# Second FFN of a fused attention and two-FFN kernel: how its w_out part is interleaved, which engine takes the low parts, and where the last y tiles and late weight parts lie

## The chip, the core and the metric

One Trainium2 chip, one core. The time of a run is the device time of the whole program in microseconds (us); lower is better. Engines are named as in the profile: PE (TensorE matmul), PEld (its weight load), DVE (VectorE), ACT (ScalarE), POOL (GpSimd), SP (SyncE, which issues nearly all DMAs here).

## What is computed

```python
# attention on keys and values averaged over 8 rows, then:
def _moe_ref(x, w_in, w_out):                       # 4608 tokens, 512 -> 2048 -> 512
    h = x @ w_in
    g = np.maximum(0.01 * h, h)
    return (g @ w_out).astype(np.float32)

def _moe2_ref(x, w_gate, w_val, w_out, rms_g):      # 4608 tokens, 512 -> 1536 -> 512
    rms = np.sqrt(np.mean(x * x, axis=-1, keepdims=True) + 1e-06)
    xn = x / rms * rms_g
    g = xn @ w_gate
    silu = g * (1.0 / (1.0 + np.exp(-g)))
    val = xn @ w_val
    return (silu * val @ w_out).astype(np.float32)
```

The weights arrive as 64-bit numbers and are turned into 32-bit ones in the kernel.

## The kernel before, in words

**Precision.** Every fp32 operand is kept as two fp32r parts: `split` (L95, L98) lets ACT copy the high part and lets DVE or POOL subtract it from the source for the low part. A product is three matmuls: high by high, high by low, low by high (`TERMS`).

**Stages.** Attention and the first FFN run together for five blocks of 512 tokens. The other four blocks go through the first FFN as two pairs, and all tokens go through the second FFN as five pairs of 2x512 or 2x384 tokens (512, 384, 512, 384, 512). Pairs use a scheme of seven products instead of eight (`Quad`, `Second`): the tokens' sums are built by `token_steps` (sums and parts `T`, `xa`, `xb`), the weights' sums beforehand by `unit` and `late_unit`, which make parts, store them in DRAM (`op_g`, `op_v`, `op_o`) and load them again when used.

**A second-FFN pair** (`second_ffn`). Its first half is 6 x 14 steps of `Quad` (gate and value products); a step is six matmuls and one `spot()`, and `at_spot` hangs other work on numbered spots. `a = 14 * NPAIR` = 84 is the first spot of the second half, the **w_out part**: 42 steps `k`, seven products (A11, S2, S1, S3, A12, S4, A22) of six steps each. A step is 12 matmuls of 128x256 for a 512 pair and 9 for a 384 pair. Step `k` runs `product(k)`, `pump()` (weight loads), `combine(k + 4)` (DVE sums for S3 and A22, L1405 and L1408), `prepare(k + 3)` (ACT high part, then the low part on DVE for even k and on POOL for odd k; tiles `b`), and `spot()`. The `b` tiles have four buffers, so ACT can write the high part of k + 3 once product k - 1 is done. The last step of a product also calls `finish`: the sums of its two PSUM banks (`v` after S2, `z` with two sums a bank after S3, `v` after S4, `u` after A22, copies on ACT after A11 and A12) and the stores of the output. DVE, ACT and POOL each work strictly in program order.

In the same part the next pair's `token_steps` hang on spots a+6, a+9, ... a+33: two `first`, then `sums`, `second`, `second_more` for each of two chunks, then two `third`. Their x tiles were normalised by `norm_steps` in the first half (squares, `mean`, `root` with a matmul `ms` at L1040, reciprocals, scaling).

**Where the two FFNs meet.** The last w_out pieces of the first FFN (`y_part`, L1366 on PE, evacuated to `oe` tiles at L1373 and L1375) run between the first steps of the first second-FFN pair, and so do the last two `late_unit`s (tiles `parts_o`). Both take tiles of the pool tag `e` (nine buffers), which also holds the `e1`, `e6`, `e7` and `e2` tiles of `Quad`. The slots `"o"` (four) hold the first FFN's w_out blocks until their last use.

Of the kernel before, what the change touches and what calls it, by code (L numbers as in the profile page):

```python
# [9 lines left out]
F32 = mybir.dt.float32  # L10
# [7 lines left out]
HI, LO = 0, 1  # L18
# [5 lines left out]
def pooled_attention_then_two_ffns(  # L24
# [685 lines left out]
    ready = set()  # L710

    def side_steps():
# [123 lines left out]
        freed = []  # L836

        def late_unit(begin, n, name, out, src, srcs_of, zs):
# [12 lines left out]
            def high(i):  # L851
                held[i] = []
                for o, (x, dst) in enumerate(srcs_of(held["raw"])[i]):
                    a, b = x.shape[1:]
                    halves = [(x, dst)]
                    if b == 512:
                        halves = [
                            (x[:, :, c:c + 2 * P], dst.rearrange("p a (h n) -> p a h n", h=2)[:, :, :, c:c + 2 * P])
                            for c in (0, 2 * P)
                        ]  # L860
                    for k, (x, dst) in enumerate(halves):
                        t = p2.tile([P, 512], F32R, tag="e", bufs=9, name=f"parts_{name}_{i}_{o}_{k}")
                        d = t[:, :2 * a * x.shape[2]].rearrange("p (a h n) -> p a h n", a=a, h=2)
                        held[i].append((x, d, dst))
                        nc.scalar.activation(out=d[:, :, HI, :], in_=x, func=AF.Copy)
# [131 lines left out]
    def norm_steps(q):  # L997
# [8 lines left out]
        for z in range(2):  # L1006
# [51 lines left out]
            steps += [lambda c=c, f=square: f(c) for c in range(KC)] + [wait, mean, wait, wait, root, wait]  # L1058
# [300 lines left out]
    def y_part(q, z, f, ms):  # L1359
# [3 lines left out]
        for m in ms:  # L1363
# [6 lines left out]
            if f == blocks(q, z)[-1]:  # L1370
                t = e_tile(N, f"oe{q}_{z}_{m}")
                if m % 2:
                    nc.scalar.copy(out=t, in_=pt)  # L1373
                else:
                    nc.vector.tensor_copy(out=t, in_=pt)  # L1375
                nc.sync.dma_start(out=y_dram[j][:, m, :], in_=t)

    class Second:


        def __init__(self, q):
# [6 lines left out]
            self.e = {}  # L1388

# [20 lines left out]
        def prepare(self, k):  # L1410
# [12 lines left out]
            split(nc.scalar, t[:, HI, :], nc.gpsimd if k % 2 else nc.vector, t[:, LO, :], src)  # L1423

        def product(self, k):
            w, x, f = self.steps[k]
            to = {"A11": "x", "A12": "x", "S1": "w", "S4": "w"}.get(w, "y")
# [16 lines left out]
            if f == HF - 1:  # L1444
                for i in range(2):
                    self.finish(w, i, self.banks[to][i][:, :2 * P * min(2, nm - 2 * i)])
# [6 lines left out]
        def finish(self, w, i, pt):  # L1453
            n = pt.shape[1]
            e = self.e
            if w == "A11":
                nc.scalar.copy(out=self.tile("u", i, n), in_=pt)
            elif w == "S2":
                add(self.tile("v", i, n), pt, e["u", i])
            elif w == "S3":  # L1460
                add(self.tile("z", i, n), pt, e["u", i])
                add(e["z", i], self.banks["w"][i][:, :n], e["z", i])
                self.store(1, 1, i, e["z", i])
            elif w == "A12":
                nc.scalar.copy(out=self.tile("c", i, n), in_=pt)
                self.store(0, 0, i, e["c", i])
            elif w == "S4":
                add(e["v", i], pt, e["v", i])
                self.store(0, 1, i, e["v", i])
            elif w == "A22":  # L1470
                add(e["u", i], pt, e["u", i])
                self.store(1, 0, i, e["u", i])
# [246 lines left out]
    def second_ffn(q):  # L1719
# [16 lines left out]

        n = 0
# [19 lines left out]
        early, late = token_steps(q + 1, xs, True) if more else ([], [])  # L1757
        for k, f in enumerate(early + late):
            put(a + 6 + 3 * k, f)
        for k in range(len(second.steps)):  # L1760
# [4 lines left out]
            spot()  # L1765
        assert not at_spot

    for q, kind in enumerate(kinds):
# [3 lines left out]
        else:  # L1772
            second_ffn(q)
# [41 lines left out]
```

## Time and profile before

| | |
|---|---|
| median of 3 runs | 1819.7 us (1812.56 to 1821.94) |
| the profiled execution's own time | 1818.55 us |
| its span, first to last instruction | 1816.8 us |
| PE busy | 1738.1 us, 96% of the span |
| DVE, ACT, POOL busy | 62%, 43%, 40% |
| mean granted TensorE clock | 0.987 of full speed |

Busy time counts an instruction from its start to its end, also while it stands still for something inside it, so a busy engine need not be a working one. Matmul ends are modelled; their starts are better for measuring distances. In waits, `PE yo <- DVE b` means that PE sat idle until DVE had written `b`.

### The profile page before, as it was taken

What the parts mean: (1) busy time and instruction counts of PE and PEld (TensorE: products, weight loads), DVE (VectorE), ACT (ScalarE), POOL (GpSimd) and SP (SyncE); (2) the same over time, 40 slices, a digit from 0 to 9 for tenths busy, and PEclk for the clock granted to TensorE, in tenths of its full rate; (3) what the DMA queues carried; (4) which work ended last, traced back from release to release, by engine and by line L of the source; (5) the groups of instructions that cost most, each with busy time, mean ns of one, the idle gap of its engine ahead of it and who ended that gap; (6) DMA issues with size and microseconds to landing.
All of it is one profiled execution on the core that took longest, in us unless ns stands there. A gap on an engine that the chain in (4) does not pass through costs nothing.

```text
span 1816.8 us, 26931 instructions
## 1 busy us (share of the span) xinstructions
PE 1738.1 (96%) x9412; PEld 1518.6 (84%) x9412; DVE 1132.5 (62%) x1901; ACT 775.3 (43%) x1646; POOL 724.9 (40%) x842
## 2 busy tenths in 40 slices
PE   6899999999999999999999998999899989989999
PEld 5799888888888888777787888999788989978889
DVE  7984555655557444475675657577755765693455
ACT  5664444454454444444453324334332434341133
POOL 5632334555432133443463334334432533351144
PEclk9899999999999999999999999999999999999999
DMA  7543655556676599979896565768565657765563
GB/s 246 198 142 111 229 194 176 176 156 215 207 224 199 172 330 321 355 246 352 289 315 223 189 225 177 241 234 280 181 227 193 213 181 267 271 211 187 177 234 114
DMA packets 227446, 403.39 MB, mean 222 GB/s; under 512 B 59120, under 2 KB 137456, under 8 KB 226800
## 3 DMA queue, kind: packets, MB, share of 16 engines
q1 hardware_dynamic: 227312, 401.67, 66.2%
q8 instruction: 75, 1.23, 0.3%
q14 instruction: 59, 0.48, 0.1%
HBM read 320.34 MB, written 81.26 MB: 221 GB/s over the span
## 4 chain that ended last, share of the span: by engine, by line
PE 72%; DVE 14%; DMA 5%; ACT 3%; issue 2%; POOL 2%; SPq 1%; ACTq 0%; DVEq 0%; POOLq 0%
PE y L642 11%; PE h L597 10%; PE o L1366 7%; PE yv L1260 5%; PE yg L1260 5%; PE wv L1260 4%; PE xo L1436 4%; PE wg L1260 4%; PE yo L1436 4%; PE xg L1260 4%; PE xv L1260 3%; PE yh L1260 3%; PE wh L1260 2%; DVE b L98 2%; PE sc L322 2%
## 5 line engine op out<-in xcount | busy, mean ns | idle before, releaser
L597 PE MATMUL h<-xhl,w_i 128*128 128x512 f32 (+1 forms) x996 | 252.8, 396 | 4.7 <-DVE ghl L620 4.7
L597 PEld LDWEIGHTS h<-xhl,w_i 128*128 128x128 f32 x996 | 178.3, 192 | 35.3 <-DVE ghl L620 5.2
L98 POOL TENSOR_TENSOR b<-u,b 128x512 fp32r<-128x512 f32 (+1 forms) x90 | 125.4, 1398 | 97.9 <-ACT b L95 97.9
L95 ACT ACTIVATE b<-u 128x512 fp32r<-128x512 f32 (+1 forms) x180 | 102.6, 585 | 125.2 <-DVE u L1405 32.8
L642 PE MATMUL y<-ghl,w_o 128*128 128x256 f32 (+1 forms) x768 | 154.4, 346 | 0.0
L1292 POOL TENSOR_TENSOR u<-e7v,e7g 128x512 f32<-128x512 f32 (+1 forms) x30 | 39.6, 1319 | 264.6 <-DVE e7v L1236 159.7
L642 PEld LDWEIGHTS y<-ghl,w_o 128*128 128x128 f32 x768 | 118.2, 192 | 12.8
L620 DVE TENSOR_TENSOR ghl<-h,ghl 128x512 fp32r<-128x512 f32 (+1 forms) x83 | 55.6, 670 | 87.3 <-ACT h L101 87.2
L642 PE MATMUL y<-ghl,wr 128*128 128x512 f32 x384 | 103.0, 404 | 0.0
L1366 PE MATMUL o<-u,wo 128*128 128x512 f32 x384 | 96.4, 390 | 0.0
L1436 PE MATMUL yo<-ao_S,b 128*128 128x256 f32 x648 | 86.8, 292 | 9.8 <-DVE b L98 7.9
L1436 PE MATMUL xo<-ao_A,b 128*128 128x256 f32 x648 | 85.0, 292 | 9.6 <-DVE b L98 9.5
L1366 PE MATMUL o<-ug,wo 128*128 128x512 f32 x384 | 89.8, 390 | 4.6 <-DMA wo<-wo 2.1
L1436 PEld LDWEIGHTS yo<-ao_S,b 128*128 128x128 f32 x648 | 82.0, 197 | 13.5 <-DVE b L98 9.9
L1436 PEld LDWEIGHTS xo<-ao_A,b 128*128 128x128 f32 x648 | 82.9, 199 | 11.5 <-DVE b L98 10.8
L1284 ACT ACTIVATE e7g<-e7g 128x512 f32<-128x512 f32 (+1 forms) x30 | 17.7, 591 | 174.6 <-DVE e7g L1236 174.6
L98 DVE TENSOR_TENSOR b<-u,b 128x512 fp32r<-128x512 f32 (+1 forms) x90 | 70.3, 783 | 31.1 <-ACT b L95 31.1
L1366 PEld LDWEIGHTS o<-ug,wo 128*128 128x128 f32 x384 | 71.7, 188 | 21.1 <-issue 2.5
L1366 PEld LDWEIGHTS o<-u,wo 128*128 128x128 f32 x384 | 72.4, 189 | 15.2
L1260 PE MATMUL yv<-T,av 128*128 128x512 f32 (+1 forms) x360 | 83.8, 368 | 0.0
L1260 PE MATMUL xg<-xa,ag 128*128 128x512 f32 (+1 forms) x360 | 83.7, 367 | 0.0
L1260 PE MATMUL yg<-T,ag 128*128 128x512 f32 (+1 forms) x360 | 83.7, 367 | 0.0
(209 smaller groups left out, 4112.2 us busy)
## 6 DMA issues: line engine op xcount, KB each, us to landing
ag<-op_g SPq DMA_DIRECT2D x90, 512.0 KB
av<-op_v SPq DMA_DIRECT2D x90, 512.0 KB
ao_S<-op_o SPq DMA_DIRECT2D x60, 512.0 KB
wo<-wo SPq DMA_DIRECT2D x52, 512.0 KB
ao_A<-op_o SPq DMA_DIRECT2D x45, 512.0 KB
wr<-wo SPq DMA_DIRECT2D x32, 512.0 KB
ah<-op_h SPq DMA_DIRECT2D x32, 512.0 KB
k<-in_k_dram SPq DMA_DIRECT2D x40, 256.0 KB
```

Source lines behind the costliest of these rows:

```text
L95: nc.scalar.activation(out=hi, in_=src, func=AF.Copy)
L98: lo_eng.tensor_tensor(out=lo, in0=src, in1=hi.bitcast(F32), op=ALU.subtract)
L322: nc.tensor.matmul(pt[:, i * n:(i + 1) * n], y[:, p, :], kblk[b % 2][:, p * n:(p + 1) * n], start=True, stop=True,)
L597: nc.tensor.matmul(pt, w[:, sp, c * P:(c + 1) * P], x[c][:, mp, c0:c1], start=c == 0 and i == 0, stop=c == KC - 1 and i == 2,)
L620: nc.vector.tensor_tensor(out=t[:, LO, :], in0=pt, in1=t[:, HI, :].bitcast(F32), op=ALU.subtract)
L642: nc.tensor.matmul(pt, w[:, sp, m * P:(m + 1) * P], g[:, mp, a - c0:a - c0 + n], start=ydone[j, a] == 1 and i == 0 and m % per_bank == 0, ...
L1260: nc.tensor.matmul(pt, wt[:, a, c, sp, :], xt[:, mp, :], start=start and c == 0 and i == 0, stop=c == 1 and i == 2, skip_group_check=not s ...
L1284: nc.scalar.activation(out=dst, in_=src, func=AF.Silu)
L1292: eng.tensor_tensor(out=t, in0=src, in1=silu[i, j], op=ALU.mult)
L1366: nc.tensor.matmul(pt, w[:, sp, m * P:(m + 1) * P], u[:, mp, :], start=f == blocks(q, z)[0] and i == 0, stop=f == blocks(q, z)[-1] and i == 2,
L1436: nc.tensor.matmul(pt, u[:, sp, m * P:(m + 1) * P], wt[:, :, mp, :], start=first and f == 0 and i == 0 and m % 2 == 0, stop=f == HF - 1 an ...
```

## The change

1. `prepare` gives the low part to POOL unless `k % 3 == 0`: 28 of 42 instead of 21.
2. `finish` is taken apart into single sums or copies. `evacuations(k)` returns them, and they go one a step on the spots after the product (only the last product's follow at once).
3. The ten token steps move: the first chunk's `sums` goes ahead of the w_out part (a-20), the others to a+1, 4, 8, 11, 21, 28, 31, 34, 38.
4. `norm_steps` gets two more empty steps between `mean` and `root`.
5. The last y tiles before the second FFN share two `ghl` tiles instead of four of tag `e`; late weight parts that are made in the second FFN go into slots `"o"`.

```diff
+                two = slot("o", late_at[0], f"parts_{name}_{i}") if in_second[0] else None
+                late_at[0] += 1
...
-                        t = p2.tile([P, 512], F32R, tag="e", bufs=9, name=f"parts_{name}_{i}_{o}_{k}")
+                        if two is None:
+                            t = p2.tile([P, 512], F32R, tag="e", bufs=9, name=f"parts_{name}_{i}_{o}_{k}")
+                        else:
+                            t = two[:, o, :]
...
-            steps += [lambda c=c, f=square: f(c) for c in range(KC)] + [wait, mean, wait, wait, root, wait]
+            steps += [lambda c=c, f=square: f(c) for c in range(KC)] + [wait, mean, wait, wait, wait, wait, root, wait]
...
-                t = e_tile(N, f"oe{q}_{z}_{m}")
+                if z and kinds[q + 1] == 2:
+                    if m % 2 == 0:
+                        both[q, m] = per.tile([P, 2, N], F32, tag="ghl", bufs=3, name=f"oe{q}_{z}_{m}")
+                    t = both[q, m - m % 2][:, m % 2, :]
+                else:
+                    t = e_tile(N, f"oe{q}_{z}_{m}")
...
+            self.FINISH = {
+                "A11": (self.copy_u,), "S2": (self.sum_v,), "S1": (), "S3": (self.sum_z, self.sum_zw),
+                "A12": (self.copy_c,), "S4": (self.sum_vw,), "A22": (self.sum_uy,),
+            }
...
-            split(nc.scalar, t[:, HI, :], nc.gpsimd if k % 2 else nc.vector, t[:, LO, :], src)
+            split(nc.scalar, t[:, HI, :], nc.gpsimd if k % 3 else nc.vector, t[:, LO, :], src)
...
-            if f == HF - 1:
-                for i in range(2):
-                    self.finish(w, i, self.banks[to][i][:, :2 * P * min(2, nm - 2 * i)])
+        def evacuations(self, k):
+            w, _, _ = self.steps[k]
+            if k % HF < HF - 1:
+                return []
+            nm = self.n // P
+            return [
+                lambda f=f, i=i, pt=self.banks[self.to(w)][i][:, :2 * P * min(2, nm - 2 * i)]: f(i, pt)
+                for i in range(2) for f in self.FINISH[w]
+            ]
...
+            def token_step(k):
+                if not tokens:
+                    early, late = token_steps(q + 1, xs, True)
+                    tokens.extend(early[2:3] + early[:2] + early[3:] + late)
+                tokens[k]()
+
+            for k, i in enumerate((-20, 1, 4, 8, 11, 21, 28, 31, 34, 38)):
+                put(a + i, token_step, k)
...
-        early, late = token_steps(q + 1, xs, True) if more else ([], [])
-        for k, f in enumerate(early + late):
-            put(a + 6 + 3 * k, f)
...
+            left = second.evacuations(k)
+            if k + 1 == len(second.steps):
+                while left:
+                    left.pop(0)()
+            for i, f in enumerate(left):
+                put(n + i, f)
```

How the instructions move is shown at three places, all in the first second-FFN pair. First POOL at the start of its w_out part (`b_k` is the low part of step k, `u_10` and `u_11` the last tiles of the first half); before, then now:

```order
L1292 TENSOR_TENSOR u_11_10689<-e1v_5_10634,e1g_5_10625 128x512
L98 TENSOR_TENSOR b_1_10735<-u_1_9928,b_1_10735 128x512
L1292 TENSOR_TENSOR u_10_10708<-e6v_5_10652,e6g_5_10643 128x512
L98 TENSOR_TENSOR b_3_10779<-u_3_10094,b_3_10779 128x512
L98 TENSOR_TENSOR b_5_10811<-u_5_10247,b_5_10811 128x512
```

```order
L1299 TENSOR_TENSOR u_11_10688<-e1v_5_10633,e1g_5_10624 128x512
L98 TENSOR_TENSOR b_1_10734<-u_1_9924,b_1_10734 128x512
L1299 TENSOR_TENSOR u_10_10707<-e6v_5_10651,e6g_5_10642 128x512
L98 TENSOR_TENSOR b_2_10761<-u_2_10109,b_2_10761 128x512
L98 TENSOR_TENSOR b_4_10795<-u_4_10259,b_4_10795 128x512
L98 TENSOR_TENSOR b_5_10813<-u_5_10239,b_5_10813 128x512
```

`b_2` was a DVE instruction and now stands on POOL behind `u_10`; POOL takes two low parts in a row, DVE every third.

Second DVE around the end of S3 (`zo` are the sums of S3, `T` and `xst` the next pair's token sums and parts); before, then now:

```order
L98 TENSOR_TENSOR b_24_11159<-u_6_10426,b_24_11159 128x512
L1079 TENSOR_TENSOR T_3_1_11162<-xst_1_9970 128x384
L1079 TENSOR_TENSOR xst_1_9970<-xst_1_9970,xst_0_9893 128x384
L1079 TENSOR_TENSOR T_3_1_11163<-xst_1_9970 128x384
L1236 TENSOR_TENSOR zo_0_11194<-yo_0_10870,uo_0_10860 128x512
L1236 TENSOR_TENSOR zo_0_11194<-wo_0_10977,zo_0_11194 128x512
L1236 TENSOR_TENSOR zo_1_11198<-yo_1_10871,uo_1_10862 128x512
L1236 TENSOR_TENSOR zo_1_11198<-wo_1_10978,zo_1_11198 128x512
L98 TENSOR_TENSOR b_26_11204<-u_8_10569,b_26_11204 128x512
```

```order
L98 TENSOR_TENSOR b_24_11153<-u_6_10416,b_24_11153 128x512
L1086 TENSOR_TENSOR T_3_1_11156<-xst_1_9965 128x384
L1086 TENSOR_TENSOR xst_1_9965<-xst_1_9965,xst_0_9889 128x384
L1086 TENSOR_TENSOR T_3_1_11157<-xst_1_9965 128x384
L98 TENSOR_TENSOR b_27_11205<-u_9_10544,b_27_11205 128x512
L1243 TENSOR_TENSOR zo_0_11208<-yo_0_10870,uo_0_10887 128x512
L1243 TENSOR_TENSOR zo_0_11208<-wo_0_10984,zo_0_11208 128x512
L1243 TENSOR_TENSOR zo_1_11244<-yo_1_10871,uo_1_10906 128x512
L98 TENSOR_TENSOR b_30_11260<-u_6_10416,b_30_11260 128x512
L1243 TENSOR_TENSOR zo_1_11244<-wo_1_10985,zo_1_11244 128x512
```

The four sums stood together ahead of `b_26`; now they stand behind `b_27`, with `b_30` among them, and `b_26` is on POOL.

Third ACT where the FFNs meet (`parts_o` are the late weight parts, `oe` the last y tiles); before, then now:

```order
L1301 COPY e1v_0_9824<-xv_0_9817 128x512
L865 ACTIVATE parts_o_0_0_0_0_9832<-raw_o_0_9649 128x2x128
L865 ACTIVATE parts_o_0_0_1_0_9834<-raw_o_0_9649 128x2x128
L1373 COPY oe_1_1_9854<-o_1_1_9437 128x512
L865 ACTIVATE parts_o_0_1_0_0_9859<-raw_o_0_9649 128x2x128
L865 ACTIVATE parts_o_0_1_1_0_9861<-raw_o_0_9649 128x128
L1373 COPY oe_1_3_9881<-o_1_3_9455 128x512
```

```order
L1308 COPY e1v_0_9824<-xv_0_9817 128x512
L872 ACTIVATE parts_o_0_0_9832<-raw_o_0_9649 128x2x128 x2
L1385 COPY oe_1_0_9847<-o_1_1_9437 128x512
L872 ACTIVATE parts_o_0_1_9857<-raw_o_0_9649 128x2x128
L872 ACTIVATE parts_o_0_1_9857<-raw_o_0_9649 128x128
L1385 COPY oe_1_2_9872<-o_1_3_9455 128x512
```

The order on ACT is the same; four `parts_o` tiles are now halves of two slots, and `oe` 1 and 3 lie in the second halves of the tiles of 0 and 2.

## Rows read from the trace of the kernel before

**Rows 1.** Waits of PE over the span: who, total us, times, longest.
```profile
PE yo L1436 <- DVE b L98: 12.1, 14, 1.8
PE xo L1436 <- DVE b L98: 9.5, 4, 3.6
PE yo L1436 <- POOL b L98: 3.4, 4, 0.9
PE wo L1436 <- DVE b L98: 2.3, 4, 0.8
PE ms L1040 <- ACT ahl L95: 1.5, 4, 0.5
PE ms L1040 <- DVE ahl L98: 1.4, 5, 0.4
```

**Rows 2.** Timeline of PE in w_out parts, last pair, then first pair: start, us.
```profile
1752.24 8.86 PE L1436 MATMUL xo<-ao_A,b 128*128 128x256 f32 x72
1804.13 8.80 PE L1436 MATMUL yo<-ao_A,b 128*128 128x256 f32 x72
...
1127.56 7.38 PE L1436 MATMUL xo<-ao_A,b 128*128 128x256 f32 x47 [3.62 <-DVE b L98]
```

**Rows 3.** Busy by window: length, PE, PEld, DVE, ACT, POOL, PEclk, DMA, GB/s.
```profile
1083.31:1154.16 70.85, 64.30 (x505) 62.52 (x504) 55.14 (x62) 32.13 (x59) 36.96 (x26) 0.98 0.62 198
1245.15:1303.16 58.01, 50.62 (x379) 47.71 (x379) 49.78 (x62) 28.40 (x59) 33.53 (x26) 0.97 0.71 240
...
1129.00:1133.00 4.00, 4.00 (x24) 4.00 (x23) 2.35 (x4) 2.09 (x4) 1.50 (x2) 0.59 0.64 214
...
977.40:987.40 10.00, 7.51 (x25) 5.71 (x26) 7.09 (x12) 5.02 (x9) 4.00 (x5) 0.83 1.05 387
```

**Rows 4.** Timeline of DVE and POOL, first pair's w_out part, its start.
```profile
1084.12 0.68 DVE L98 TENSOR_TENSOR b<-u,b 128x512 fp32r<-128x512 f32 x1
1086.43 1.78 DVE L1398 TENSOR_TENSOR t<-u,u 128x512 f32<-128x512 f32 x1
...
1084.35 1.61 POOL L1292 TENSOR_TENSOR u<-e6v,e6g 128x512 f32<-128x512 f32 x1 [0.16 <-DVE e6v L1236]
1085.92 3.45 POOL L98 TENSOR_TENSOR b<-u,b 128x512 fp32r<-128x512 f32 x2
1090.10 1.29 POOL L98 TENSOR_TENSOR b<-t,b 128x512 fp32r<-128x512 f32 x1 [0.72 <-ACT b L95]
```

**Rows 5.** Timeline of the second pair's w_out part (384 tokens): DVE, POOL, ACT.
```profile
1284.04 1.01 DVE L98 TENSOR_TENSOR b<-u,b 128x384 fp32r<-128x384 f32 x2
1285.01 1.75 DVE L98 TENSOR_TENSOR T<-T,T 128x512 fp32r<-128x512 f32 x1
1286.68 1.50 DVE L1079 TENSOR_TENSOR xst<-xst,T 128x512 f32<-128x512 f32 x1
1288.10 0.55 DVE L98 TENSOR_TENSOR b<-u,b 128x384 fp32r<-128x384 f32 x1
...
1250.57 1.02 POOL L98 TENSOR_TENSOR b<-t,b 128x384 fp32r<-128x384 f32 x1 [0.68 <-ACT b L95]
1284.54 1.68 POOL L98 TENSOR_TENSOR xa<-xst,xa 128x512 fp32r<-128x512 f32 x1 [1.57 <-ACT xa L95]
1286.17 1.46 POOL L98 TENSOR_TENSOR b<-u,b 128x384 fp32r<-128x384 f32 x1
...
1283.41 0.53 ACT L95 ACTIVATE b<-u 128x384 fp32r<-128x384 f32 x1 [1.89 <-PE xo L1436]
```

**Rows 6.** Timeline of DVE, first pair, end of S3.
```profile
1123.53 0.68 DVE L1236 TENSOR_TENSOR zo<-yo,uo 128x512 f32<-128x512 f32 x1
```

**Rows 7.** Timeline where the FFNs meet.
```profile
976.66 0.69 DVE L1236 TENSOR_TENSOR e7g<-yg,e1g 128x512 f32<-128x512 f32 x1 [5.96 <-DMA y<-oe]
980.80 0.69 DVE L1236 TENSOR_TENSOR e7v<-yv,e1v 128x512 f32<-128x512 f32 x1 [2.12 <-DMA op_o<-parts_o]
981.55 2.45 PE L1260 MATMUL yv<-xb,av 128*128 128x512 f32 x6 [2.48 <-DVE e7v L1236]
```

More of the change, by code (lines that the diff above doesn't have):

```diff
@@ L710, in pooled_attention_then_two_ffns @@
     ready = set()
+    in_second = [False]
     def side_steps():
@@ L836, in side_steps @@
         freed = []
+        late_at = [0]
         def late_unit(begin, n, name, out, src, srcs_of, zs):
@@ L1388, in __init__, with to @@
             self.e = {}
+            self.FINISH = {
+                "A11": (self.copy_u,), "S2": (self.sum_v,), "S1": (), "S3": (self.sum_z, self.sum_zw),
+                "A12": (self.copy_c,), "S4": (self.sum_vw,), "A22": (self.sum_uy,),
+            }
+        def to(self, w):
+            return {"A11": "x", "A12": "x", "S1": "w", "S4": "w"}.get(w, "y")
         def t1(self, f):
@@ L1422, in prepare @@
             t = self.ready[k] = t[:, :, :self.n]
-            split(nc.scalar, t[:, HI, :], nc.gpsimd if k % 2 else nc.vector, t[:, LO, :], src)
+            split(nc.scalar, t[:, HI, :], nc.gpsimd if k % 3 else nc.vector, t[:, LO, :], src)
         def product(self, k):
             w, x, f = self.steps[k]
-            to = {"A11": "x", "A12": "x", "S1": "w", "S4": "w"}.get(w, "y")
+            to = self.to(w)
             first = w in ("A11", "S2", "S1")
@@ L1451, in tile, with copy_u, sum_v, sum_z @@
             return t
[L1453 to L1472, printed above, removed]
+        def copy_u(self, i, pt):
+            nc.scalar.copy(out=self.tile("u", i, pt.shape[1]), in_=pt)
+        def sum_v(self, i, pt):
+            add(self.tile("v", i, pt.shape[1]), pt, self.e["u", i])
+        def sum_z(self, i, pt):
+            add(self.tile("z", i, pt.shape[1]), pt, self.e["u", i])
+        def sum_zw(self, i, pt):
+            z = self.e["z", i]
+            add(z, self.banks["w"][i][:, :z.shape[1]], z)
+            self.store(1, 1, i, z)
+        def copy_c(self, i, pt):
+            nc.scalar.copy(out=self.tile("c", i, pt.shape[1]), in_=pt)
+            self.store(0, 0, i, self.e["c", i])
+        def sum_vw(self, i, pt):
+            add(self.e["v", i], pt, self.e["v", i])
+            self.store(0, 1, i, self.e["v", i])
+        def sum_uy(self, i, pt):
+            add(self.e["u", i], pt, self.e["u", i])
+            self.store(1, 0, i, self.e["u", i])
         def store(self, h, z, i, t):
@@ L1735, in second_ffn @@
             put(a - 5 + 2 * k, second.prepare, k)
+        if more:
+            tokens = []
+            def token_step(k):
[5 more added lines that the diff above has]
+                put(a + i, token_step, k)
         n = 0
@@ L1772, in pooled_attention_then_two_ffns @@
         else:
+            in_second[0] = True
             second_ffn(q)
```

## The prediction

> **What bounds the kernel now.** PE does: it is busy for 96% of the span, so only time in which it stands still or runs slowly is to be had. I read the list of PE's waits first [rows 1]: 27.3 us are waits for the low parts `b` of the w_out parts, 2.9 us waits of the `ms` matmuls for their `ahl` tile. The list has no other row of the second FFN except the two places of [rows 7].
>
> Next, PE's timeline of these parts [rows 2]. The last pair has no next pair and no wait: six products start 51.89 us apart in all, 8.65 each, so a whole part of seven is 60.5 us, a step 1.44, a matmul 0.12. A 384 pair has 9 matmuls a step: 1.08 a step, 45.4 a part. The windows [rows 3] give 70.85 for a 512 part with a next pair and 58.01 for a 384 part, which is 10.3 and 12.6 us too long. There are two of each (their twins agree within 0.1), **45.9 us in all**. That is more than the waits, because the clock falls: in 1129 to 1133 us it is 0.59 of full speed (that is, 1.2 instead of 2.4 GHz for most of it), right after PE sat idle for 3.62 us [rows 2], and 4 x 0.41 = 1.6 us are lost.
>
> Why the low parts are late is seen in the timeline of DVE and POOL [rows 4]. `t<-u,u` takes 1.78 us on DVE where a subtraction of the same size takes 0.68, and it stands inside POOL's two subtractions (1085.92 to 1089.37). In [rows 5] it can be followed to the end: DVE's pair ends at 1285.05, POOL's `xa` at 1286.22, DVE's `T` at 1286.76, POOL's `b` at 1287.63, DVE's `xst` at 1288.18, DVE's `b` at 1288.65. Each ends one fixed time after the other engine's. So a subtraction with both sources in SBUF and a POOL instruction take turns, and **both engines share one queue**. Its prices, when full, are 1.17 on POOL and 0.55 on DVE for 128x512, 0.87 and 0.47 for 128x384. Sums that read PSUM are not held up (`zo`, 0.68 [rows 6]).
>
> **The change, part by part.** I keep a ledger of that queue over blocks of steps: what it is given, less the steps' time on PE, carried on, and never below zero.
>
> *Slack.* The low part of step k + 3 can begin when product k - 1 is done and ACT has written the high part. For 384 that leaves 3 x 1.08 + 0.12 (only the second matmul needs it) - 0.53 for ACT [rows 5] - 0.87 - two hand-overs of 0.1 = 1.7 us; for 512, with ACT's 0.53 scaled to the width (0.7), about 2.4.
>
> *Before, 384, as a trial.* Up to step 11 nothing piles up. The sums after S2 make DVE wait for that product's end: 1.7 behind at step 12. Steps 12 to 19: eight low parts 5.4, six sums for S3 2.8, token steps `sums` 1.65, `second` 1.7, `second_more` 2.3, against 8.64: 6.9 behind. Steps 20 to 31: low parts 8.0, token steps 6.7, the four sums `zo` in a row 2.0 (two are half as wide) with POOL idle, against 12.96: 10.7. Steps 32 to 37: 4.0 + 2.8 + 1.1 + 1.0 against 6.48: 13.1. Less the slack 11.4; the window says 12.6 - 1.6 = 11.0. For 512 the same ledger gives 6.4 where 10.3 - 1.6 = 8.7 stand: 2.3 short.
>
> *Now, 384.* Six steps bring four low parts on POOL and two on DVE, 4.4. Steps 0 to 7: 5.8 + two `t` sums 0.9 + two `first` 1.1, under 8.64. Steps 8 to 13: 4.4 + `second` 1.7 + `second_more` 2.3 against 6.48: 1.9 behind. Steps 14 to 19: 4.4 + 2.8: 2.7. Steps 20 to 27: 5.8 + `sums` 1.65 against 8.64: 1.5. Steps 28 to 31: 3.1 + 1.1 + 2.3 against 4.32: 3.6. Steps 32 to 37: 4.4 + 2.8 + `third` 1.7: 6.1. Less the slack, **4.4 us late**. Every moved low part costs the queue more (0.87 for 0.47, seven times 2.8 us); what helps is that no sum waits for a product's end, that the `zo` sums come one a step while POOL works, and that the tokens leave steps 12 to 20 alone. With half a chance of a fall of the clock (0.8) I take 5.2: 7.4 saved, two times, **14.8**.
>
> *Now, 512.* The same blocks (8.64, with 384-wide tokens) give 0.3, 0.7, 0, 1.05 and 2.8 behind, 0.4 late after the slack. I add the 2.3 by which the trial was short: 2.7, no fall of the clock. Saved 10.3 - 2.7 = 7.6, two times, **15.2**. Bounds: 0.4 and, with a fall, 4.3.
>
> *The start of each part.* `b_2` now stands on POOL behind `u_10`. That starts at 1084.35 [rows 4]; with 1.29 for each, `b_2` is there at 1086.9, while its matmul is due 25 matmuls after 1083.31 [rows 3], at 1086.3. PE is 0.6 late (0 to 1.4, if DVE steps between). In parts with token steps it is inside the lateness above; in the last pair it is new: **0.6 lost**.
>
> *Where the FFNs meet.* DVE's `e7g` and `e7v` stand 5.96 and 2.12 us for DMAs out of tiles of tag `e`, and PE waits 2.48 for the second [rows 7]. The window around it has PE busy 7.51 of 10 us at a clock of 0.83 [rows 3]: 2.5 idle + 1.7 at the lower clock. With `oe` and the last `parts_o` elsewhere, those tiles were stored long before: **4.2 saved** (bounds 0 and 4.6).
>
> *The `ms` matmuls.* Two more steps before each: their 2.9 us of waits [rows 1] go but for some 0.5, **2.4 saved**.
>
> *At nothing.* `sums` at a-20 puts three DVE sums (0.55 each) between the gate and value products; PE waits for DVE nowhere there, and if that cover were gone it costs 1.7 a pair. Normalisation ends four spots later, at spot 57, still ahead of a-20. ACT does the same work, its copies `uo` and `co` a step later each. On SP the output stores stand among the next pair's weight loads and wait for DVE; behind them stand loads that wait for PE's release anyway, and a load that is late next would show as a wait of PE for `ag` or `av`. The `ghl` tiles of `oe` wait for the last pieces' own tiles, done before.
>
> Sum: 14.8 + 15.2 + 4.2 + 2.4 - 0.6 = 36.0. The profiled execution took 1818.55, which is 1.15 under the median of the three runs, so within what they differ by. **1818.5 - 36 = 1782.5 us.**
>
> **Rivals.**
> *The full price.* In the queue each instruction might hold the other engine up for its whole length: 1.29 and 0.68 [rows 4], 1.02 and 0.55 [rows 5]. The ledger now ends at 13.3 and 7.7 behind, 11.7 and 5.4 late, with the clock 12.5 and 6.2; saved 0.1 and 4.1, two times each, + 4.2 + 2.4 - 0.6 = 14.4: 1804. Against it: the same prices make the 384 part of before 18 us late instead of 11, and in [rows 5] the ends lie closer together than these lengths. The Trainium skill (SBUF — State Buffer, "Who interferes with whom") says just this: a DVE instruction with two SBUF inputs contends with a GpSimd instruction that reads SBUF, and the loser is blocked for the whole instruction; by its letter the time is 1804. The trace agrees on who is blocked, not on the price.
>
> *Two free engines.* If turn-taking mattered little, DVE's relief would empty all parts: 45.9 + 4.2 + 2.4 - 0.6 = 51.9, 1766.6. Against it stands the 1.78 of [rows 4].
>
> *Slower: the queue is full throughout.* If it never drains, spreading gains nothing and each moved low part adds its difference: 7 x 0.62 in three 512 parts and 7 x 0.40 in two 384 parts, 18.6, and 0.6, less 6.6 for the other two places: 1831. It decides once prices are some 15% higher, since steps 0 to 7 and 20 to 27 then no longer fit into 8.64. For it: [rows 5] shows a stretch without a gap. Against it: those steps hold 7.8 and 7.4 by these prices. The Trainium skill (GPSIMD Engine Reference, its opening) calls GpSimd the wrong choice for ordinary elementwise arithmetic, VectorE being about twice as fast; 1.29 against 0.68 agrees.
>
> *The new buffers wait too.* The slots `"o"` still hold w_out blocks that PE's last pieces read, so ACT's `parts_o` can wait for PE, and `oe`, the silu and DVE stand behind it. Then the change doesn't remove that wait: 4.2 back, 1786.7.
>
> **How the numbers follow.** My forecast 0.68, new buffers 0.08, full price 0.10, two free engines 0.07, full queue 0.07. The range takes in the bounds (512 parts 0.4 to 4.3 late, 384 parts 4.4 without a fall of the clock and 6.0 with one, the meeting place 0 to 4.6 saved), the free engines at its low end and the full price at its high end: 1767 to 1805. About 0.5%, 9 us, is what can be told from no change: all cases but the full queue are faster by more, and that one, at 1831, lies just past the line; I leave 0.03 for no change.
>
> **What would show it.** In the profile after: the waits of PE for `b` fall from 27 to some 10 us, most of it in the 384 parts and after step 30; 512 parts of about 63 us and 384 parts of about 50.5; the last pair's part 0.6 longer, with a wait for POOL's `b` in its third step; no wait of PE for `e7v`; `ms` waits near nothing; POOL's busy time up, and DVE's sums still stretched inside POOL's. Wrong it would be if 384 parts stay above 56 us, if PE waits for POOL over the whole part, or if the gate and value products wait for DVE.

## The result, and the profile after

The changed kernel takes **1799.8 us** (median of 4 runs, 1796.52 to 1800.92) where the kernel before takes 1819.62 (4 runs, 1812.56 to 1821.94): the ratio is 0.9895, with a 95% interval of 0.9864 to 0.9925. The profiled execution took 1796.52 us, its span is 1794.5. So the change gains about 20 us, of 36 forecast.

PE's list of waits (who, total us, times, longest), to be held against [rows 1]:

```profile
PE yo L1456 <- POOL b L98: 8.7, 8, 1.6
PE yg L1267 <- DVE e6g L1243: 5.5, 3, 1.9
...
PE xo L1456 <- POOL b L98: 4.4, 5, 0.9
...
PE wo L1456 <- DVE b L98: 2.6, 4, 0.9
PE xo L1456 <- DVE b L98: 2.5, 2, 1.2
```

The waits for `b` fall from 27.3 to 18.2 us (these four rows; two smaller ones hold 1.3 more), and over two thirds of them are now for POOL. The `ms` rows are gone. A row that was not there before has come: 5.5 us for DVE's `e6g`, in gate and value products.

The windows (length, PE, PEld, DVE, ACT, POOL, PEclk, DMA, GB/s) of a 512 part, a 384 gate and value stretch and a 384 part, answering to [rows 3]:

```profile
1076.56:1141.10 64.54, 61.57 (x505) 60.72 (x504) 53.51 (x52) 32.67 (x59) 46.54 (x33) 1.00 0.68 213
1141.10:1233.58 92.48, 88.92 (x510) 88.08 (x509) 57.51 (x99) 29.57 (x54) 25.87 (x24) 1.00 0.74 251
1233.58:1288.00 54.42, 47.95 (x379) 45.91 (x379) 46.96 (x52) 29.05 (x59) 40.70 (x33) 1.00 0.76 255
```

Parts of 64.54 and 54.42 us stand against 70.85 and 58.01 before, and against no-stall lengths of 60.5 and 45.4. The clock is 1.00 in them, where it was 0.98 and 0.97. The second 384 gate and value stretch, of 92.56 us, has 0.98.

All stretches of the first pair, then the next, from PE's first matmul of each, make the balance (us, after less before): 512 parts -12.6 in both together, 384 parts -7.1, the last part +1.1, the first gate and value stretch (where the FFNs meet) -5.1, the two 384 stretches +3.0, the first FFN's pairs -2.1, attention +0.4. Together, but for rounding, -22.3, the difference of the spans.

PE's timeline in the last product of the first 384 part and at the start of the last part ([rows 2] has the latter before, without a wait):

```profile
1277.79 0.39 PE L1456 MATMUL yo<-ao_A,b 128*128 128x256 f32 x1 [0.44 <-ACT b L95]
...
1282.68 3.58 PE L1456 MATMUL yo<-ao_A,b 128*128 128x256 f32 x27 [1.63 <-POOL b L98]
1286.96 1.21 PE L1456 MATMUL yo<-ao_A,b 128*128 128x256 f32 x8 [0.70 <-POOL b L98]
...
1728.83 3.15 PE L1456 MATMUL xo<-ao_A,b 128*128 128x256 f32 x25
1732.89 5.89 PE L1456 MATMUL xo<-ao_A,b 128*128 128x256 f32 x47 [0.91 <-POOL b L98]
```

The first three rows belong to the last product (steps 36 to 41), where the largest single share of a 384 part's lateness arises. Its first matmul starts at 1277.79, 44.2 us behind the part's start at 1233.58, where six products with no stall take 38.9: 5.3 us late. At the part's end it is 9.0. The rest came bit by bit: 1.0 at the start, the remainder from the third product on. The wait after 25 matmuls in the last part is the third step's low part on POOL; it stands at the start of all five parts (five waits of `xo` for POOL in the list).

What DVE, POOL and ACT do ahead of these two waits (timeline of each, start and us):

```profile
1267.01 0.68 DVE L1243 TENSOR_TENSOR zo<-yo,uo 128x512 f32<-128x512 f32 x1
1267.72 0.69 DVE L1243 TENSOR_TENSOR zo<-wo,zo 128x512 f32<-128x512 f32 x1
1268.33 0.41 DVE L1243 TENSOR_TENSOR zo<-yo,uo 128x256 f32<-128x256 f32 x1
...
1275.14 1.48 DVE L1086 TENSOR_TENSOR xst<-xst,T 128x512 f32<-128x512 f32 x1 [1.18 <-POOL xa L98]
1276.55 1.01 DVE L1428 TENSOR_TENSOR u<-u,t 128x384 f32<-128x384 f32 x2
...
1278.76 1.46 DVE L98 TENSOR_TENSOR xb<-xst,xb 128x512 fp32r<-128x512 f32 x1
1280.14 2.90 DVE L1428 TENSOR_TENSOR u<-u,t 128x384 f32<-128x384 f32 x2
...
1268.99 1.09 POOL L98 TENSOR_TENSOR b<-u,b 128x384 fp32r<-128x384 f32 x1 [2.32 <-ACT b L95]
...
1278.28 1.39 POOL L98 TENSOR_TENSOR b<-u,b 128x384 fp32r<-128x384 f32 x1 [2.20 <-ACT b L95]
1279.63 1.73 POOL L98 TENSOR_TENSOR xb<-xst,xb 128x512 fp32r<-128x512 f32 x1
1281.32 1.31 POOL L98 TENSOR_TENSOR b<-u,b 128x384 fp32r<-128x384 f32 x1
...
1277.21 0.99 ACT L95 ACTIVATE b<-u 128x384 fp32r<-128x384 f32 x2 [3.33 <-DVE u L1428]
```

Three `zo` sums still come in a row, since DVE is late, and POOL stands 2.32 us meanwhile, for a high part of ACT. Further on DVE stands 1.18 us because its sum overwrites the `xst` that POOL's `xa` still reads; ACT stands 3.33 us for the sums `u` behind it, and POOL 2.20 for ACT. Then two sums `u` take 2.90 us beside POOL's `xb` and `b`, where the pair before took 1.01. Laid over each other, the rows of the two engines from 1266 us to the part's end at 1288.01 leave 2.7 us in which neither has an instruction in the queue and 2.9 in which POOL alone has.

The gate and value products of a 384 pair, where the new waits are (timeline of DVE, ACT, PE):

```profile
1192.39 0.69 DVE L98 TENSOR_TENSOR ahl<-acc,ahl 128x512 fp32r<-128x512 f32 x1 [5.92 <-ACT ahl L95]
1193.00 0.55 DVE L1243 TENSOR_TENSOR e6g<-yg,e1g 128x384 f32<-128x384 f32 x1
...
1191.73 0.63 ACT L95 ACTIVATE ahl<-acc 128x512 fp32r<-128x512 f32 x1 [2.85 <-POOL acc L1038]
...
1193.60 1.32 PE L1267 MATMUL yg<-T,ag 128*128 128x384 f32 x6 [1.93 <-DVE e6g L1243]
```

`mean`'s subtraction on DVE waits for ACT and through it for POOL's sum of squares `acc`; `e6g`, which frees a PSUM bank, stands behind it, and PE waits for that. On DVE this `mean` stood just ahead of the same `e6g` before, too:

```profile
1203.14 0.82 DVE L98 TENSOR_TENSOR ahl<-acc,ahl 128x512 fp32r<-128x512 f32 x1 [2.83 <-ACT ahl L95]
1203.88 0.54 DVE L1236 TENSOR_TENSOR e6g<-yg,e1g 128x384 f32<-128x384 f32 x1
```

Then DVE stood 2.83 us for it and PE waited for `ms` alone. In the changed kernel it stands 5.92 us, because the squares come later against PE's work: ACT starts them 1.8 us ahead of the product that this `e6g` sums, where it was 6.5 before. This is one wait of 1.93 us in each 384 stretch. The third `e6g` wait, 1.63 us in the first stretch, comes later, where DVE is at reciprocals and scalings of the normalisation.

### The profile page after: what moved, and what is told of

Read it like the earlier page. It is cut to its first block, busy times and chain, and to the rows that moved or that the text cites. A ratio compares the mean times of both kernels' runs of the same rounds, so it can differ in the third digit from the quotient of the medians.

```text
span 1794.5 us, 26922 instructions
## 1 busy us (share of the span) xinstructions
PE 1720.8 (96%) x9412; PEld 1507.7 (84%) x9412; DVE 1135.4 (63%) x1866; ACT 776.4 (43%) x1646; POOL 759.6 (42%) x877
## 4 chain that ended last, share of the span: by engine, by line
PE 74%; DVE 11%; DMA 5%; POOL 3%; ACT 3%; issue 2%; SPq 1%; ACTq 0%; POOLq 0%; DVEq 0%
PE y L642 11%; PE h L597 10%; PE o L1373 7%; PE yg L1267 6%; PE yv L1267 6%; PE yo L1456 4%; PE xg L1267 4%; PE xv L1267 4%; PE wv L1267 4%; PE wg L1267 4%; PE yh L1267 3%; PE xo L1456 3%; PE wo L1456 2%; PE sc L322 2%; PE wh L1267 2%
## 5 line engine op out<-in xcount | busy, mean ns | idle before, releaser
L98 POOL TENSOR_TENSOR b<-u,b 128x512 fp32r<-128x512 f32 (+1 forms) x120 | 163.3, 1371 | 67.0 <-ACT b L95 63.6
L1456 PE MATMUL xo<-ao_A,b 128*128 128x256 f32 x648 | 81.1, 284 | 6.9 <-POOL b L98 4.4
L1456 PEld LDWEIGHTS xo<-ao_A,b 128*128 128x128 f32 x648 | 79.1, 191 | 8.5 <-POOL b L98 5.4
L1267 PE MATMUL xv<-xa,av 128*128 128x512 f32 (+1 forms) x360 | 83.7, 367 | 0.0
L1456 PE MATMUL wo<-ao_S,b 128*128 128x256 f32 x648 | 80.9, 284 | 2.9 <-DVE b L98 2.6
L1456 PEld LDWEIGHTS wo<-ao_S,b 128*128 128x128 f32 x648 | 78.8, 192 | 4.1 <-DVE b L98 3.5
```

Source lines behind the costliest of these rows:

```text
L98: lo_eng.tensor_tensor(out=lo, in0=src, in1=hi.bitcast(F32), op=ALU.subtract)
L1267: nc.tensor.matmul(pt, wt[:, a, c, sp, :], xt[:, mp, :], start=start and c == 0 and i == 0, stop=c == 1 and i == 2, skip_group_check=not s ...
L1456: nc.tensor.matmul(pt, u[:, sp, m * P:(m + 1) * P], wt[:, :, mp, :], start=first and f == 0 and i == 0 and m % 2 == 0, stop=f == HF - 1 an ...
```

## The experiments

The main theory is that of the prediction: DVE and POOL share one queue, so a low part moved to POOL costs, and the gain comes from where sums and token steps stand in the order of the engines. The main rival is relief: DVE is what PE waited for, and giving it less is the gain. Twelve kernels ran; the first four edit the changed kernel. The time is that of the profiled execution. Lengths are from PE's first matmuls; Q is a 384 gate and value stretch, W a w_out part, both shown as first and second, and "W all" the sum of the five parts (276.3 with no stall: 2 x 60.5, 2 x 45.4 and, for the last, which is measured to PE's end, 64.5).

| kernel | time | span | 512 W | 384 Q | 384 W | last W | W all |
|---|---|---|---|---|---|---|---|
| before | 1818.55 | 1816.8 | 70.85, 70.81 | 90.99, 91.00 | 58.01, 58.00 | 64.46 | 322.1 |
| changed | 1796.52 | 1794.5 | 64.54, 64.53 | 92.48, 92.56 | 54.42, 54.47 | 65.57 | 303.5 |
| x1_all_dve | 1773.27 | 1771.6 | 60.47, 60.47 | 92.81, 93.15 | 46.85, 46.85 | 64.48 | 279.1 |
| x2_b2_dve | 1794.39 | 1792.3 | 63.39, 63.40 | 92.99, 92.50 | 53.56, 54.05 | 64.42 | 298.8 |
| x3_norm_back | 1797.96 | 1796.3 | 64.57, 64.56 | 91.02, 90.77 | 54.93, 54.49 | 65.58 | 304.1 |
| x4_half | 1782.68 | 1781.0 | 61.53, 61.53 | 92.46, 93.42 | 51.33, 51.31 | 64.47 | 290.2 |
| y1_sums | 1799.27 | 1797.6 | 64.31, 64.38 | 90.75, 90.75 | 55.07, 54.93 | 64.48 | 303.2 |
| y2_tokens | 1800.75 | 1799.0 | 64.25, 64.25 | 91.13, 91.67 | 55.71, 55.22 | 64.49 | 303.9 |
| y3_low | 1819.26 | 1817.5 | 69.28, 69.28 | 90.75, 90.75 | 60.21, 60.03 | 65.57 | 324.4 |
| y4_all_dve | 1791.62 | 1789.9 | 62.07, 62.20 | 90.73, 91.15 | 52.49, 52.50 | 64.47 | 293.7 |
| z1_norm | 1769.51 | 1767.8 | 60.47, 60.47 | 91.13, 91.59 | 46.85, 46.85 | 64.47 | 279.1 |

Times of single runs differ by some us (before: 1812.56 to 1824.12 over all its runs), the twins within one trace mostly by 0.1 to 0.5, so what follows rests on the stretches. The other three kernels, z2, z3 and v1, stand with their runs below.

**x1_all_dve**: every low part of the w_out part on DVE.

```diff
-            split(nc.scalar, t[:, HI, :], nc.gpsimd if k % 3 else nc.vector, t[:, LO, :], src)
+            split(nc.scalar, t[:, HI, :], nc.vector, t[:, LO, :], src)
```

> The changed kernel with every low part b of the w_out parts on DVE, none on GpSimd; all else as changed. In the changed kernel the w_out parts with a next pair last 64.5 us (512 tokens) and 54.4 us (384), where 60.5 and 45.4 are without any stall. Theory of the shared queue (two-source SBUF subtractions of DVE and GpSimd take turns, and GpSimd's are the dearer, 0.87 for 0.47 and 1.17 for 0.55): the queue is given less, six steps of a 384 part 2.8 instead of 4.4 us, so the parts shrink to about 61 and 47 us, the wait for b in the third step goes, and the span falls by some 20 us. Theory of relief (DVE is the short engine, and what the change gained came from its seven low parts that went to GpSimd): DVE gets 28 instructions of 0.55 or 0.68 us more in each part, and the 384 parts go back beyond the 58 us of before, the span above 1805 us.

512 parts without any stall and 384 parts 1.45 us from it: 24.4 us less in the five parts than the changed kernel. Relief falls. Windows of x1_all_dve, then its low parts by form (busy, mean ns | idle before), and the same groups of the changed kernel:

```profile
1077.19:1137.66 60.47, 60.47 (x506) 60.47 (x505) 50.77 (x79) 32.68 (x59) 8.90 (x5) 1.00 0.75 230
1230.47:1277.32 46.85, 46.06 (x380) 45.54 (x379) 43.67 (x79) 29.16 (x59) 8.51 (x6) 1.00 0.87 293
...
L98 DVE TENSOR_TENSOR b<-u,b 128x384 fp32r<-128x384 f32 x72 | 39.9, 572 | 1.5 <-ACT b L95 1.5
```

```profile
L98 POOL TENSOR_TENSOR b<-u,b 128x384 fp32r<-128x384 f32 x48 | 58.7, 1234 | 22.6 <-ACT b L95 19.4 <-DMA out_dram<-co 2.2 <-DMA ag<-op_g 0.7
L98 DVE TENSOR_TENSOR b<-u,b 128x384 fp32r<-128x384 f32 x24 | 20.6, 858 | 3.7 <-ACT b L95 3.7
```

DVE is busy for less time in a 384 part with 79 instructions (43.67) than it was with 52 (46.96). With POOL out of the way one of its low parts takes 572 ns in place of 858: it had spent the difference standing inside POOL's. That POOL is merely the slower engine, with nothing shared, would not shorten DVE's own instructions.

**x4_half**: the changed kernel with part 1 undone.

```diff
-            split(nc.scalar, t[:, HI, :], nc.gpsimd if k % 3 else nc.vector, t[:, LO, :], src)
+            split(nc.scalar, t[:, HI, :], nc.gpsimd if k % 2 else nc.vector, t[:, LO, :], src)
```

> The changed kernel with low parts on GpSimd for odd steps only, as before (21 of 42 instead of 28). Theory of the shared queue: seven low parts go back to the cheaper engine, six steps of a 384 part bring 4.0 instead of 4.4 us; the ledger gives 2 us less for a 384 part (52.4), 61 to 62.5 for a 512 part and 1.1 less for the last part, some 9 us in all. Theory of relief: DVE gets seven more and the parts grow by 2 to 3 us each.

Parts of 61.53 and 51.3: part 1 of the change costs 3.0 us in a 512 part, 3.1 in a 384 part, 1.1 in the last, 13.3 in all, where some 9 were expected. The whole gain in the parts is that of parts 2 and 3 (part 4 leaves them as they are: x3_norm_back, 304.1 for 303.5).

**x2_b2_dve**: only step 2's low part, the one behind POOL's `u_10`, back on DVE.

```diff
-nc.gpsimd if k % 3 else nc.vector
+nc.gpsimd if k % 3 and k != 2 else nc.vector
```

> The changed kernel with the third low part of each w_out part (b_2) on DVE again. If the 0.9 us wait for it at the start of each of the five parts is simply lost time, each part is 1.1 us shorter, the span 5.5 us. If the shared queue sets when the parts end, the start only moves the waiting to later steps: then the last part, which has no token steps, is 1.1 us shorter and the four others keep their 64.5 and 54.4 us within 0.4 us.

The 512 parts and the last one are 1.1 us shorter, the 384 parts 0.9 and 0.4 (the second of these at a clock of 0.97). So the wait at the start is time lost by itself, on top of the lateness later in the part; for the 384 parts that holds in part. The span is only 2.2 us shorter, since the first FFN's pairs took 1.8 us more.

**x3_norm_back**: the two empty steps of part 4 out again.

```diff
-[wait, mean, wait, wait, wait, wait, root, wait]
+[wait, mean, wait, wait, root, wait]
```

> The changed kernel without the two more empty steps between mean and root. In the changed kernel the gate and value stretch of the 384 pairs is 92.5 us long, 91.0 before, though its ms waits (1.35 us) are gone. Theory that the longer normalisation moved the second mean and scaling to steps where DVE holds up e6g: the stretch is 91.0 us again, with ms waits back, and the span 3 us shorter. Theory that the sums at a-20 hold up DVE there: the stretch gets longer still, about 93.9 us, since the ms waits come back on top.

The 384 stretches are back at 91.0 and 90.8; `e6g` waits go and 3.4 us of `ms` waits return. So part 4, meant for those waits, made these two stretches 1.5 and 1.8 us longer. The span, expected 3 us shorter, is 1.8 longer all the same: the first FFN's pairs take 345.1 us in this run and 340.7 in the changed kernel.

The next four put one part of the change, or its opposite, into the kernel before. **y1_sums** has part 2 alone (the hunks of `finish` and `evacuations`), **y2_tokens** part 3 alone (the token steps' spots), **y3_low** part 1 alone:

> The kernel before with part 2 of the change alone (sums of finish one a step on the spots after the product). Shared queue (sums that read PSUM leave the queue half empty when four stand together, and no sum makes DVE wait for a product's end at once): about a third to a half of the lateness goes; 384 parts 53 to 54 us from 58.0, 512 parts 63 to 65 from 70.8, last part unchanged at 64.5, span 1792 to 1797. Rival, spreading hardly matters and the change's gain came from DVE's relief and the token steps: 384 parts over 56, 512 parts over 68, span over 1808.

Parts of 64.3 and 55: as expected, the 384 parts a little over. The clock is 0.97 in them, which is 1.6 us of their lateness.

> The kernel before with part 3 of the change alone (the next pair's token steps at their new spots). Shared queue: steps 12 to 20, where low parts and the sums for S3 already fill the queue, lose six token steps, and the queue starts the last third almost empty; 384 parts 50 to 51 us from 58.0, 512 parts 61.5 to 63 from 70.8, last part 64.5 (it has no token steps), span about 1785. Rival, the amount of work counts and not its place: parts within 2 us of before, span over 1810. In either case no 384 gate and value stretch grows, since the empty steps of the normalisation are not in it (it does if the first token sum ahead of the part is what makes them longer in the changed kernel).

64.25 and 55.2 to 55.7: a large gain, but less than expected (61.5 to 63 and 50 to 51). PE's and DVE's timeline shows what is left:

```profile
1252.94 4.57 PE L1436 MATMUL wo<-ao_S,b 128*128 128x256 f32 x36 [1.16 <-DVE b L98]
...
1271.95 5.80 PE L1436 MATMUL xo<-ao_A,b 128*128 128x256 f32 x35 [2.96 <-DVE b L98]
...
1269.24 0.68 DVE L1236 TENSOR_TENSOR zo<-yo,uo 128x512 f32<-128x512 f32 x1
1269.95 0.69 DVE L1236 TENSOR_TENSOR zo<-wo,zo 128x512 f32<-128x512 f32 x1
...
1271.35 1.02 DVE L98 TENSOR_TENSOR b<-u,b 128x384 fp32r<-128x384 f32 x2
```

The four sums `zo` still stand in a row ahead of `b`, and PE waits 2.96 us for it. So the order on DVE matters beside the queue's work. The gains of parts 2 and 3 overlap a little: 19.0 us in the five parts for y1, 18.2 for y2, 32.0 for both (x4_half) where their sum is 37.2.

> The kernel before with part 1 of the change alone (low parts two of three on POOL). Shared queue: each moved low part costs the queue 0.40 us (384) or 0.62 us (512) more; 384 parts 60 to 62 us from 58.0, 512 parts 73 to 75 from 70.8, last part 65.6 from 64.5 (its third low part stands behind the last u of the gate and value stretch), span 1826 to 1832. Rival, relief of DVE (PE waits for DVE's b in the list of before, so fewer on DVE is better): 384 parts under 56, 512 parts under 69, span under 1810.

384 parts of 60.2 and 60.0, as the queue theory has it (+2.1), though not all of that is waiting: PE's busy time in them is 1.1 and 0.5 us longer, at clocks of 0.94 and 0.97. The last part is 1.1 longer, as expected. The 512 parts are 1.55 us shorter, though, against 2 to 4 longer. Window of the first of them in y3_low, to be held against the first line of [rows 3]:

```profile
1082.32:1151.60 69.28, 63.12 (x506) 61.06 (x505) 55.23 (x55) 31.88 (x59) 47.67 (x33) 1.00 0.64 204
```

PE stands still for 6.16 us there and for 6.55 before, and the clock is 1.00 where it was 0.98. What was one wait of 3.62 us behind the `zo` sums is spread over several, the longest 1.65; with no fall of the clock PE's busy time is 1.2 us shorter. So in 512 parts part 1 alone neither costs nor gains much but that. Relief wanted under 69 and under 56: the 512 parts miss that by 0.28 us, the 384 parts went the other way. It falls here too.

**y4_all_dve** has every low part on DVE and nothing else.

```diff
-nc.gpsimd if k % 2 else nc.vector
+nc.vector
```

> The kernel before with every low part of the w_out part on DVE and nothing else changed. Shared queue: 21 low parts a pair cost 0.55 in place of 1.17 or 0.47 in place of 0.87; 384 parts about 51 us from 58.0, 512 parts 61 to 63 from 70.8, last part 64.5, span 1783 to 1790. Rival, relief of DVE: DVE, which PE waits for in before, becomes the bound; 384 parts over 60, 512 parts over 73, span over 1830.

62.1 and 52.5: 28.4 us less in the parts than before, by one line, more than the change's five parts give (18.6). The 384 parts are 1.5 over what was expected. The rival wanted longer parts; it falls.

**z1_norm** and **z2_mean_late** edit x1_all_dve's normalisation; **z3_tokens_dve** adds the tokens' low parts.

```diff
-[wait, mean, wait, wait, wait, wait, root, wait]
+([wait, mean, wait, wait, root, wait] if kinds[q - 1] == 2 else [wait, mean, wait, wait, wait, wait, root, wait])
```

> The kernel of x1_all_dve with part 4 of the change (two empty steps before root) kept only in the first FFN; in the second FFN the steps are those of before. If the 384 gate and value stretches are longer because the empty steps put the second mean just ahead of e6g, where DVE in program order waits for ACT's ahl: stretches 91.0 from 92.8 and 93.2 us, waits of PE for e6g gone, some 2 us of waits of ms back in their place, parts unchanged at 60.5 and 46.9, span about 1768. Rival, the token sums ahead of the part or the low parts on DVE make the stretch longer: it stays at 92.8 to 93.2, span 1771.

91.1 and 91.6, no `e6g` wait, 2.7 us of `ms` waits, span 1767.8: as the first theory said, and as in x3_norm_back.

```diff
-[wait, mean, wait, wait, wait, wait, root, wait]
+[wait, wait, wait, wait, mean, wait, wait, root, wait]
```

> The kernel of x1_all_dve with mean three steps later after the squares (four empty steps ahead of it, two between it and root). If DVE's wait at mean is for POOL's sum of squares, which is done some three steps after the last square, nobody waits any more: no wait of PE for e6g or ms, 384 gate and value stretches 89.5 to 90 us from 92.8 and 93.2, 512 stretches 115.0, span 1764 to 1766, device time about 1767 against 1773 of x1_all_dve. Rival, reciprocals and scaling, which now end two spots later, hold up e6g and e7g instead: stretches 91 to 93, span 1768 to 1772.

No wait for `e6g` is left and none for `ms` in the second FFN (one of 0.5 us stands in the first), and the stretches are 1 us shorter than expected, PE busy all the time. `mean` now stands behind that `e6g` on DVE. Window of the first:

```profile
1136.37:1224.82 88.45, 88.45 (x510) 88.08 (x509) 58.17 (x100) 29.57 (x54) 25.83 (x23) 1.00 0.76 259
```

Time: 1764.27 us (1762.7 to 1768.31, 5 runs), 0.9705 of before (0.9687 to 0.9724).

```diff
-nc.gpsimd if done[0] % 3 == 0 else nc.vector
+nc.gpsimd if done[0] % 3 == 0 and kinds[q - 1] == 1 else nc.vector
```

> The kernel of z2_mean_late with the token steps' low parts in the second FFN on DVE too, so that POOL does next to nothing in the w_out parts. Shared queue: a 128x512 low part costs 0.55 on DVE in place of 1.17 on POOL; the last waits of the 384 parts go, 46.9 to 45.4 to 46.2 us, 512 parts stay at 60.5, span 1 to 3 us under z2_mean_late. Rival, DVE is full (busy 43.7 of 46.9 us in a 384 part of x1_all_dve): 384 parts 47.5 us and more, span over that of z2_mean_late.

384 parts of 46.31 from 46.84: shorter, as expected, but just short of the 46.2 that was the least expected. The rival, a full DVE, falls. The span, expected 1 to 3 us under z2's, is 1761.4 against 1761.2: the first FFN's pairs took 0.9 us more in this run. Time: **1762.65 us** (1760.41 to 1764.36, 4 runs), 0.9690 of before (0.9673 to 0.9707). Whether z3 gains over z2 can't be told by time, since the two intervals overlap; z2 and z3 both beat the changed kernel, whose ratio is 0.9895 (0.9864 to 0.9925).

**v1_parts_back**: the changed kernel with the late weight parts in tag `e` again, the y tiles still in `ghl`.

```diff
-                two = slot("o", late_at[0], f"parts_{name}_{i}") if in_second[0] else None
+                two = slot("o", late_at[0], f"parts_{name}_{i}") if False else None
```

> The changed kernel with the late weight parts in tiles of tag e again (the other half of part 5, the last y tiles in ghl, stays). If the transfers out of parts_o are what DVE's e7v waits for, the wait of PE for e7v comes back, alone or with a fall of the clock: first gate and value stretch 122.5 to 125 us from 120.4, span 1797 to 1799. Rival, taking the four y tiles out of the tag is enough, because the buffers then come round later and the transfers have ended: the stretch stays at 120.4, no wait for e7v, span 1794 to 1795.

The stretch stays at 120.41 us; the span is 1796.3, with 1.9 us more in the first FFN's pairs. DVE's timeline:

```profile
973.17 0.69 DVE L1243 TENSOR_TENSOR e7g<-yg,e1g 128x512 f32<-128x512 f32 x1 [3.72 <-issue]
976.64 0.69 DVE L1243 TENSOR_TENSOR e7v<-yv,e1v 128x512 f32<-128x512 f32 x1 [1.46 <-DMA op_o<-parts_o]
```

DVE still waits for the transfer out of `parts_o`, 1.46 us instead of 2.12 [rows 7], but `e7g` waits for no transfer and ran earlier, so PE doesn't notice. The four y tiles out of the tag are enough; the first expectation falls. The other half alone, `parts_o` moved and the y tiles not, wasn't run.

## Why the prediction was right and wrong

The time lies in the range, and in the w_out parts the mechanism is the one forecast; in the gate and value stretches it is not. The sum was too large by some 14 us against the spans (36.0 and 22.3): the 384 parts fell short of it by 7.7, `ms` by 5.4, the 512 parts by 2.6, the start by 0.5, while the meeting place gave 0.9 more and the first FFN 2.1 that nobody forecast. The 384 parts and the meeting place lie outside the bounds given for them. With the bounds of its own terms alone the range would have ended near 1792 (over the forecast 2 x 1.6 in 512 parts, 2 x 0.8 in 384 parts, 4.2 and 0.8). It held because it reached up to the rival's 1804, and that is luck. By its steps:

*512 parts*, forecast 15.2 saved, measured 12.6 (4.0 late instead of 2.7). The step that failed is "in parts with token steps it is inside the lateness above": the wait for `b_2` came on top. With that wait taken out (x2_b2_dve) the parts are 63.4, 2.9 late, as the sum has it. Of its 2.7, though, the ledger gives 0.4; the other 2.3 are what the trial lacked, carried over without a mechanism.

*384 parts*, forecast 14.8 saved, measured 7.1 (9.0 late instead of 4.4). The ledger, "*Now, 384*", is the step that failed. Its price of the moved low parts can't be the cause: it gave seven times 0.40, 2.8 us, and undoing the move (x4_half) gives 3.1, the wait at the start included. That wait is 0.4 to 0.9 of the 4.6 by which the parts are later than the ledger has them. What it left out is that the engines work in program order and wait for each other: it reckons the queue as working whenever something is behind, at its full price. In the last 22 us of the part the queue is empty for 2.7 us (1.6 of it during the three `zo` sums in a row, which the ledger had "one a step while POOL works"), and POOL works alone, at 1.01 to 1.09 a low part instead of 0.87, for 2.9. That this makes up the rest of the 4.6 us is argued from the timeline; no run took these waits away by themselves. Half a chance of a fall of the clock was 0.8 too much: there was none.

*The start of each part*, forecast 0.6 once, in the last part: measured 1.1 there, within the bounds 0 to 1.4. But the wait stands in all five parts and costs 1.1 in the 512 parts too, 0.4 to 0.9 in the 384 parts (x2_b2_dve).

*Where the FFNs meet*, forecast 4.2, measured 5.1, over the upper bound of 4.6. The mechanism was right and the wait is gone; the clock's share was larger than the window showed (5.1 less the 2.9 us of PE's waits leaves 2.2). Of the two buffers moving `oe` is enough (v1_parts_back); whether moving `parts_o` alone is, no run shows.

*The `ms` matmuls*, forecast 2.4 saved. The waits went, but the two 384 stretches are 3.0 us longer together, by waits for `e6g`. The step that failed is "PE waits for DVE nowhere there": the forecast looked at what `sums` at a-20 would hold up and not at the second `mean`, which stands ahead of `e6g` on DVE and comes two spots later, since the first `root` has two more empty steps ahead of it. With two steps fewer (x3_norm_back, z1_norm) or with `mean` behind `e6g` (z2_mean_late) these waits are gone. `sums` at a-20, put at nothing, cost little: with part 3 alone (y2_tokens) the stretches are 91.1 and 91.7, where they were 91.0. This is one of the signs that the prediction named as showing it wrong.

*The first FFN's pairs*, not forecast: 340.7 from 342.7. In the six traces with the old steps they take 342.4 to 345.1 us, in the eight with part 4's steps or the later `mean` 340.6 to 342.5, so most of it seems to be part 4's. From 840 to 880 us the clock is 0.96 in the six, 1.00 in the eight; why isn't settled.

*The rivals.* Two free engines: 384 parts of 54 say no, and x1_all_dve, where DVE alone does better than both. Full queue throughout: spreading sums gained 6.5 us a 512 part, so no; but its price for moved low parts held roughly in the 384 parts (x4_half 3.1, y3_low 2.1, for 2.8). New buffers that wait: no such wait. The full price: its 1804 is nearer to the time than the forecast, by another route. Its parts would be 11.7 and 5.4 late; they are 9.0 and 4.0, between it and the forecast's 4.4 and 2.7, so the lengths don't decide. The ends do: in the timeline after (start and duration added), POOL's `b`, `xb` and `b` end at 1279.67, 1281.36 and 1282.63, DVE's `xb` at 1280.22 and the last `u` at 1283.04: DVE's ends follow 0.55 and 0.41 behind POOL's, and POOL's `xb` 1.14 behind DVE's, where the full price asks for 0.68, 0.55 and 1.29. The Trainium skill (SBUF — State Buffer, "Who interferes with whom") is borne out on who blocks whom; that the block lasts for the whole instruction, which the page says of this case under "SBUF: two separate sides", is not the price here. One row of the prediction could not show what it was read for: `zo` at 1123.53 [rows 6], the sum from PSUM that isn't held up, stands where POOL is idle. The fourth one does show it, with the same 0.69 us beside POOL's `b`:

```profile
1125.56 0.69 DVE L1236 TENSOR_TENSOR zo<-wo,zo 128x512 f32<-128x512 f32 x1
1125.69 1.26 POOL L98 TENSOR_TENSOR b<-u,b 128x512 fp32r<-128x512 f32 x1 [2.50 <-ACT b L95]
```

That the queue blocks at all was worth more than the prediction made of it: the sum stopped at what the change does, while the queue said that the low parts belong on DVE altogether. The Trainium skill (GPSIMD Engine Reference, its opening), which advises VectorE for ordinary elementwise arithmetic, was the better guide there; x1_all_dve and y4_all_dve agree.

## What to carry to other kernels

Where two engines take turns at one resource, moving work to the slower one to relieve the faster costs both; price a move by what it takes of the shared resource, and try putting all of it on the faster engine. A ledger of such a resource leaves out what engines in program order lose by waiting for each other; here it came out right in a trial on the kernel before (11.4 late for 11.0) and at half on the kernel after (4.4 for 9.0). Add a wait at a new place on top, not inside. Empty steps put in before one instruction delay all that follow: look at what stands behind each of them on its engine, even where the order there doesn't change.

## What the runs showed of the hardware that was not expected

DVE's busy time can fall when it is given more: 46.96 us with 52 instructions in a 384 part, 43.67 with 79, because a low part of 128x384 takes it 572 ns on average with POOL nearly idle and 858 beside POOL's. And the same idle time of PE can come with different clocks: in a 512 part 6.55 us of it, 3.62 in one wait, with 0.98, and 6.16 us, the longest wait 1.65, with 1.00. But the longest wait doesn't settle it: the two 384 parts of x3_norm_back have the same waits up to the last product's 1.61 us, and clocks of 0.97 and 1.00.
